# Weight splits of the experts without GpSimd, another order of the slots, and slots of 160 tokens, in a kernel of attention, a dense layer pair and a mixture of experts

## The chip, the cores and the metric

The kernel runs on one core of a Trainium2 chip, as one program. The metric is the time of one execution on the device in microseconds (us). The kernel before takes 613.17 us, the median of three runs (613.17, 613.51 and 611.21).

## The reference

Three layers run one after another, all in float32 with the dense layer's weights given in float64:

```python
scores = q @ k^T / 8, causal; attn = softmax(scores); x = attn @ v      # 2 x 12 heads, 448 tokens, 64 wide
x = x.reshape(896, 768)
y = (relu(x @ w_in) ** 2) @ w_out                                       # 768 -> 2048 -> 768
expert = argmax(normalized(y) @ normalized(expert_emb)^T / tau)         # one of 8 per token
gate   = softmax of the same logits, at the chosen expert
for e in range(8):
    out[expert == e] = gate * (relu(y[expert == e] @ w1[e]) @ w2[e])    # 768 -> 1024 -> 768
```

Which expert gets how many tokens is known only on the device.

## The kernel before

Products need more digits than one pass of TensorE gives, so every operand is kept as a high part (a rounded copy) and a low part (what the rounding left), and a product is made of three: high by high, high by low and low by high. The helper `copy_on` (L57 to L63) makes high parts, `lo_of` (L65, L66) low parts by a subtraction. Which engine does a class of them is a letter in the table `CFG`: A is ScalarE, V is VectorE, G is GpSimd; several letters go in turn by the piece's number.

Attention and the first dense layer take about the first half of the time. Then come seven tiles of 128 tokens of the second dense layer with their routing (`route_tile`), and as the last one goes on, the experts.

An expert's weights are 16 pieces of 128 x 768: pieces 0 to 7 for the first layer, 8 to 15 for the second. `pieces` loads two pieces at a time (768 KB, on SyncE's queue, into one of six buffers named `xraw` and `mraw`) and splits each into `mh` (high) and `ml` (low). All experts share one set of 16 slots for split pieces, so a piece of the next expert can be split only when TensorE has done with the same piece of the expert before, and its buffer is loaded again only when both parts are made. `CFG["mhi"]` names the engines of the high parts, `CFG["mlo"]` those of the low parts.

The tokens of an expert go into a slot of fixed size. The early slot (form D, 256 tokens) takes tokens of the expert that has most in the first five tiles; a slot of form M takes more of them with the same weights. After it come five static slots, `FORMS = "LMTTT"`, that hold 384 (L), 192 (M) and 64 (T) tokens, each with an expert's weights of its own, the larger ones for the experts with more tokens; `CFG["order"]` says in which order they are run. `tables` computes on the device which expert gets which slot and which token which lane. What does not fit goes to further slots of form L, which `rest` runs only if a flag says that there are tokens left.

`mm1_w` computes the first layer of forms D and M with the weights as the stationary operand, eight steps of 128 hidden units; in form M the moving operand is [high | low] of the tokens, so a step is six pairs of products (L703, L704), and VectorE then adds the two halves (`hsum`, L707) and makes the low part of the hidden layer (L712). `mm1_x` does form T (and the last third of L) with the tokens stationary: four steps of 256 hidden units; each result is added up by VectorE (`hr`, L774), transposed by TensorE (`ht`, L747), and becomes high and low part of the hidden layer (`act`, L749 on ScalarE, L750 on VectorE). `mm2` is the second layer, eight steps with two halves of 384 columns; a part with fewer than 128 tokens goes through `two_pass`, where high and low of the tokens lie side by side as one stationary operand. `mm2_out` weights the result by the gate (`osb`, L809 to L812), and GpSimd scatters it to the output with an indirect DMA (L814). `slot_x` gathers a slot's tokens (L826, GpSimd), transposes them (`xt`, L836) and splits them (`act`, L840 and L66).

The order of TensorE's work is written out by hand: `run_slot` calls hooks between the steps. On the other engines a scheduler orders the instructions when the program is built, and each engine works in that order.

Of the kernel before, what the change touches and what calls it, by code (L numbers as in the profile page):

```python
# [20 lines left out]
P = 128  # L21
# [11 lines left out]
def f32(ap):  # L33
# [5 lines left out]
    joint=1, mhi="AAAV", rt6=[1, 4, 7, 9, 15], woh="A", h2h="A", h2l="V", rt=[1, 3, 5, 7, 10], et=[9, 10, 14],  # L39
    turn2=[1, 3], ft0=[0, 1, 2, 3, 4], ft1=[3, 7], ft2=[2, 4, 5, 6], stop=0, mlo="VVGG", xh="A", h2="A",  # L40
# [4 lines left out]
    vh="AG", kl="G", vl="G", pth="AAAA", nrm="GGGGGGG", u0=1, order=[1, 2, 0, 3, 4])  # L45


def build(tc, qkd, vd, w_in, w_out, emb, tau, wm, cst, out, dbg_y=None):
# [24 lines left out]
    # causal, the same for rows 0 to 63 and 64 to 127  # L73
# [19 lines left out]
    # the activation tables come in while the first loads are under way  # L93
# [4 lines left out]
    # left: staging, slots of one f tile of weights, x (later phase B's tiles); right: attention (later h2)  # L98
# [8 lines left out]
    def w_load(src, f, slot, name, wh="wh", wl="wl", parts=1):  # L107
        """f tile of a float64 weight (as int64 words): float32 with 24 bits, then hi and lo"""
# [29 lines left out]
    # zeros that stay: beside the queries' blocks, beside v's second head, and after the even chunks  # L138
    # of the probabilities
# [29 lines left out]
    def s_prep(u):  # L169
        # rows 0 to 63: the first head of the pair; rows 64 to 127: the second  # L170
# [31 lines left out]
    # the chunks' order in each half unit  # L202
    COL = {c: i for i, c in enumerate(sum(sum(CFG["ch"], ()), ()))}

    def s_scores(u, c):
        """chunk c of the queries of both heads of a pair: the array's two diagonal blocks"""
# [27 lines left out]
    # the probabilities' transposes: blocks of 128 keys j, chunks of queries c >= 2 * j; a bank takes four  # L234
    BANKS = [[(0, c) for c in range(4)], [(0, c) for c in range(4, 7)] + [(3, 6)],
             [(1, c) for c in range(2, 6)], [(1, 6)] + [(2, c) for c in range(4, 7)]]
    # block j lies in half of them, from this chunk on
# [15 lines left out]
    def s_pv(u, j):  # L253
        """block j of the keys for both heads of a pair: the first gives rows 0 to 63, the second the others"""
# [55 lines left out]
    def scores_at(k):  # L310
        """the chunks of scores of half unit k, in three parts"""
        u = (k + 3) // 2
        return [[(units[u], c) for c in x] for x in CFG["ch"][(k + 1) % 2]] if 0 <= u < NU else [(), (), ()]
# [11 lines left out]
    # the array's clock rises with its work: products that nobody reads, while the pipeline fills  # L325
# [62 lines left out]
    def h2_split(t, q):  # L388
        """hi and lo of four f tiles of a token tile's h2, as [P, f, 128]"""
# [13 lines left out]
    # the next pieces of h2 go before the matrix products that they follow on DVE and ACT  # L403
# [27 lines left out]
    # phase B: y = h2 @ w_out for a tile of 128 tokens at a time, and its routing  # L431
# [8 lines left out]
    # unit-length expert embeddings, transposed, hi | lo  # L440
# [7 lines left out]
    def norm_of(pool, ss, n, name):  # L448
        """sqrt(ss) for [n, 1]: Newton's iteration for 1/sqrt on DVE"""
# [58 lines left out]
    def route_tile(t, y):  # L508
# [40 lines left out]
        # first of the maxima: least of (index - 8)  # L549
# [9 lines left out]
        # gate = 1 / (sum + 1e-9), in two parts  # L559
# [7 lines left out]
        # place among the tokens of its expert  # L567
# [8 lines left out]
    def lanes(rk, nt, name):  # L576
        """half and lane in a slot of 256, of ranks [P, nt]"""
# [6 lines left out]
    def table(oc, nt, nv, ncol, lane, name):  # L584
        """sum over tokens of (one-hot of the lane) x (one-hot of the column) * value"""
# [27 lines left out]
    def early():  # L613
        """the first 256 tokens of the expert with most tokens in the first NE tiles"""
# [30 lines left out]
    # the experts: pieces of [P, 768] of an expert's weights go round the 16 slots  # L645
# [9 lines left out]
    def h_at(fs, part, n, m=1):  # L655
        """hi and lo of the hidden layer of a part's n tokens (of m parts)"""
# [6 lines left out]
    def pieces(s, res):  # L663
        """the weights of an expert: 16 pieces, (hi, lo) each"""
# [21 lines left out]
    # forms of a slot: tokens of its parts. 64 tokens of one part lie with hi and lo side by side  # L686
# [39 lines left out]
    def two_pass(os, x, whs, wls, k, n):  # L726
        """x = [hi | lo] of 64 tokens: rows 0 to 63 of o get hi * (wh + wl), the others lo * wh"""
        def high():
            for o, w in zip(os, whs):
                T.matmul(o, x, w, start=(k == 0), stop=(k == n - 1))  # L730
# [368 lines left out]
NE = 5  # L1099
# [73 lines left out]
```

## Time and profile before

| | |
|---|---|
| Median of the runs | 613.17 us |
| Lowest and highest run | 611.21 and 613.51 us |
| Profiled execution: first to last instruction (span) | 610.8 us |
| Mean granted clock of TensorE | 0.968 of full |
| TensorE matmul busy | 568.2 us (93%) |
| TensorE weight loads busy (beside the matmuls) | 522.3 us (86%) |
| VectorE busy | 433.8 us (71%) |
| ScalarE busy | 274.0 us (45%) |
| GpSimd busy | 274.7 us (45%) |
| Bytes moved by DMA | 86.71 MB, 142 GB/s on average |

The profile gives the profiled execution as its span; what an execution has beyond that is not shown apart, and the lowest of the three runs lies 0.4 us above the span. Busy times are sums over the whole span, so they say nothing on which engine another waits for in a given stretch; for that one reads the windows, the timelines and the waits. In the rows PE is TensorE, PEld its weight loads, DVE VectorE, ACT ScalarE, POOL GpSimd and SP SyncE. L66 is line 66 of the kernel.

### The profile page before, as it was taken

To read this page: it belongs to the slowest core of one execution; us is meant where nothing else is said; L and a number is where in the kernel's file an instruction comes from. 1 tells how busy PE (TensorE), PEld (TensorE's weight loads), DVE (VectorE), ACT (ScalarE), POOL (GpSimd) and SP (SyncE) were. 2 spreads that over 40 slices of the span, in tenths; PEclk is the share of its full clock that TensorE was granted. 3 is DMA by queue.
4 is the path that set the end of the run, shared out by engine and by line. 5 is a ranking of instruction groups with operands and counts; after the bars stand their busy time and mean duration, and the time that the engine had idled before them with its cause. 6 is when DMAs were issued, how large, how long until landed. Compare 5 with 4: busy or idle time off the path is not lost. (4 is left out here: it accounts for less than half of the span.)

```text
span 610.8 us, 9820 instructions
## 1 busy us (share of the span) xinstructions
PE 568.2 (93%) x3501; PEld 522.3 (86%) x3501; DVE 433.8 (71%) x876; ACT 274.0 (45%) x630; POOL 274.7 (45%) x252
## 2 busy tenths in 40 slices
PE   6999999999999999999999988899898978999783
PEld 3788788899999989999999987899898957999663
DVE  6877778856779885976543779752988897265981
ACT  4776777424343425333332155103564654164541
POOL 7667577915554362210000055112574687054860
PEclk7999999999999999999999999899998969999788
DMA  7659433333364455411000192038486679047600
GB/s 223 161 134 256 112 66 93 126 105 104 103 207 156 155 166 198 156 53 52 27 27 10 34 407 94 2 133 308 155 268 212 228 240 296 3 141 257 206 1 6
DMA packets 28298, 86.71 MB, mean 142 GB/s; under 512 B 2854, under 2 KB 13094, under 8 KB 28240
## 3 DMA queue, kind: packets, MB, share of 16 engines
q1 hardware_dynamic: 26640, 79.51, 40.6%
q0 software_dynamic: 1600, 6.49, 2.9%
q8 instruction: 29, 0.48, 0.3%
q14 instruction: 29, 0.24, 0.1%
HBM read 75.44 MB, written 6.49 MB: 134 GB/s over the span
## 5 line engine op out<-in xcount | busy, mean ns | idle before, releaser
L66 POOL TENSOR_TENSOR ml<-xraw,mh 128x768 fp32r<-128x768 f32 x32 | 64.1, 2009 | 39.4 <-ACT mh L59 27.8
L215 PE MATMUL s<-kh,q 128*128 128x128 f32 (+6 forms) x168 | 51.5, 340 | 6.0 <-ACT p L219 4.5
L66 DVE TENSOR_TENSOR ml<-xraw,mh 128x768 fp32r<-128x768 f32 x32 | 48.7, 1522 | 11.7 <-ACT mh L59 11.6
L793 PE MATMUL ops<-mh,act 128*128 128x384 f32 x224 | 53.7, 342 | 0.0
L230 POOL TENSOR_SCALAR p<-p,rs 128x192 f32<-128x192 f32 (+6 forms) x84 | 43.4, 535 | 18.6 <-ACT p L219 12.7
L59 ACT ACTIVATE mh<-xraw 128x768 fp32r<-128x768 f32 x48 | 40.1, 844 | 21.9 <-PE ops L793 10.3
L264 PE MATMUL pv<-pt,v 128*128 128x448 f32 (+7 forms) x288 | 48.6, 304 | 0.0
L219 ACT ACTIVATE p<-s,mn 128x192 f32<-128x192 f32 (+6 forms) x84 | 39.6, 476 | 10.1 <-DVE mn L218 6.1
L123 DVE SCALAR_TENSOR_TENSOR w<-raw,w 128x768 int32<-128x768 int32 x32 | 43.1, 1350 | 0.7
L264 PEld LDWEIGHTS pv<-pt,v 128*128 128x128 f32 (+3 forms) x288 | 37.0, 163 | 5.2 <-issue 0.3
L215 PEld LDWEIGHTS s<-kh,q 128*128 128x128 f32 x168 | 33.8, 204 | 8.2 <-ACT p L219 5.4
L66 POOL TENSOR_TENSOR ml<-mraw,mh 128x768 fp32r<-128x768 f32 x16 | 33.2, 2082 | 15.3 <-ACT mh L59 10.6
L826 POOL DMA_INDIRECT xr<-ydram,egi x2 | 2.3, 1128 | 83.8 <-DVE esi L605 83.5
L793 PEld LDWEIGHTS ops<-mh,act 128*128 128x128 f32 x224 | 39.1, 188 | 0.3
L66 DVE TENSOR_TENSOR hs<-h,hs 128x512 fp32r<-128x512 f32 (+1 forms) x32 | 21.9, 691 | 24.7 <-ACT hs L59 24.5
L218 DVE TENSOR_REDUCE mn<-s 128x1 f32<-128x192 f32 (+6 forms) x84 | 34.1, 415 | 5.1 <-PE s L216 4.8
L121 DVE SCALAR_TENSOR_TENSOR w<-raw,w 128x768 int32<-128x768 int32 x32 | 36.0, 1128 | 0.7
L119 DVE TENSOR_SCALAR w<-raw 128x768 int32<-128x768 int32 x32 | 22.3, 698 | 18.8 <-POOL wi3l L66 6.7
L66 DVE TENSOR_TENSOR pt<-pt 128x512 fp32r<-128x512 f32 x48 | 32.4, 680 | 2.8 <-ACT pt L59 2.7
L294 ACT ACTIVATE relu<-pa 128x448 f32<-128x448 f32 x32 | 17.1, 538 | 36.6 <-PE pa L290 36.6
L703 PE MATMUL hps<-act,mh 128*128 128x384 f32 x96 | 29.5, 377 | 3.6 <-DVE hsum L707 3.6
L826 POOL DMA_INDIRECT xr<-ydram,fgi x10 | 12.0, 1197 | 44.9 <-DVE ei L999 23.5
(461 smaller groups left out, 1790.1 us busy)
## 6 DMA issues: line engine op xcount, KB each, us to landing
xraw<-in_wm SPq DMA_DIRECT2D x32, 768.0 KB, 4.5
raw<-in_w_in SPq DMA_DIRECT2D x16, 768.0 KB, 4.2
raw<-in_w_out SPq DMA_DIRECT2D x16, 768.0 KB, 4.2
mraw<-in_wm SPq DMA_DIRECT2D x16, 768.0 KB, 5.1
qk<-in_qkd SPq DMA_DIRECT2D x11, 448.0 KB, 5.2
q<-qs SPq DMA_DIRECT2D x22, 224.0 KB, 3.9
v<-in_vd SPq DMA_DIRECT2D x12, 256.0 KB, 4.1
ydram<-ysb SPq DMA_DIRECT2D x7, 384.0 KB, 2.3
```

The lines of the kernel that those rows point to most:

```text
L59: A.activation(out, in_, AF.Copy, scale=scale)
L66: eng.tensor_tensor(out=lo, in0=x, in1=hi, op=ALU.subtract)
L119: V.tensor_scalar(out=w[:, x], in0=raw[:, x, 1], scalar1=3, scalar2=0x3FFFFFFF, op0=ALU.logical_shift_left, op1=ALU.bitwise_and)
L121: V.scalar_tensor_tensor(out=w[:, x], in0=raw[:, x, 1], scalar=-0x40000000, in1=w[:, x], op0=ALU.bitwise_and, op1=ALU.bitwise_or)
L123: V.scalar_tensor_tensor(out=w[:, x], in0=raw[:, x, 0], scalar=29, in1=w[:, x], op0=ALU.logical_shift_right, op1=ALU.bitwise_or)
L215: T.matmul(ss, d["q2"][:, c, :, :, x].rearrange("p a b -> p (a b)"), d[y][:, :n], start=i == 0, stop=False)
L218: last["max"] = V.reduce_max(out=d["mn"][:, i:i + 1], in_=ss, axis=AX.X, negate=True)
L219: A.activation(d["p"][c][:, :n], ss, AF.Exp, bias=d["mn"][:, i:i + 1], accum_out=d["sm"][:, i:i + 1])
L230: G.tensor_scalar(out=p, in0=p, scalar1=rs[:, COL[c]:COL[c] + 1], scalar2=1.0, op0=ALU.mult, op1=ALU.mult)
L264: T.matmul(d["pv"][:, j * P:S] if h else d["pv"][0:D, j * P:S], d[x][0:k, j, 1:3].rearrange("p a b -> p (a b)") if h else d[x][0:k, j, 0], ...
L703: T.matmul(both, wh[:, c], mo["x"][:, kc, :, 0:n], start=(kc == 0), stop=False)
L793: T.matmul(ps[c], x, ww[:, c * 384:(c + 1) * 384], start=(fc == 0 and x is hh and ww is wh), stop=(fc == 7 and x is hl))
```

## The change

There are three edits, and nothing else that computes.

- Splits of the experts' weights: high parts (`mhi`) by ScalarE alone, where every fourth was VectorE's; low parts (`mlo`) by VectorE alone, where half were GpSimd's. GpSimd keeps the gathers and scatters of the experts.
- The static slots come in the order T, M, T, L, T, where it was M, T, L, T, T.
- Form M holds 160 tokens, where it held 192: its second part has 32 tokens instead of 64. `two_pass` and `mm2_out` take the number of tokens, the table of gates for the low rows is made for 32 as well as 64, and slot sizes are counted in units of 32.

```diff
-    joint=1, mhi="AAAV", ...
+    joint=1, mhi="A", ...
-    turn2=[1, 3], ..., stop=0, mlo="VVGG", xh="A", h2="A",
+    turn2=[1, 3], ..., stop=0, mlo="V", xh="A", h2="A",
-    vh="AG", kl="G", vl="G", pth="AAAA", nrm="GGGGGGG", u0=1, order=[1, 2, 0, 3, 4])
+    vh="AG", kl="G", vl="G", pth="AAAA", nrm="GGGGGGG", u0=1, order=[2, 1, 3, 0, 4])
...
-    FORM = dict(D=(P, P), M=(P, 64), S=(P,), T=(64,))
+    FORM = dict(D=(P, P), M=(P, 32), S=(P,), T=(64,))
...
-    def two_pass(os, x, whs, wls, k, n):
+    def two_pass(os, x, whs, wls, k, n, m):
         def high():
             for o, w in zip(os, whs):
-                T.matmul(o, x, w, start=(k == 0), stop=(k == n - 1))
+                T.matmul(o[0:2 * m], x, w, start=(k == 0), stop=(k == n - 1))
...
-            T.matmul(o[0:64], x[:, 0:64], w, start=False, stop=False)
+            T.matmul(o[0:m], x[:, 0:m], w, start=False, stop=False)
...
-                A.activation(oc, ps[c][64:P], AF.Copy, scale=s[1][3][64:P, col:col + 1])
-                V.scalar_tensor_tensor(out=oc, in0=ps[c][0:64], scalar=gate[0:64, col:col + 1], in1=oc,
+                A.activation(oc, ps[c][n:2 * n], AF.Copy, scale=s[1][3][n:2 * n, col:col + 1])
+                V.scalar_tensor_tensor(out=oc, in0=ps[c][0:n], scalar=gate[0:n, col:col + 1], in1=oc,
...
-        V.tensor_copy(gate2[64:P], gate[0:64])
+        for n in (64, 32):
+            V.tensor_copy(gate2[n:2 * n], gate[0:n])
...
-SIZE = dict(L=384, M=192, T=64)
+SIZE = dict(L=384, M=160, T=64)
+UNIT = 32
```

How the order moves shows on VectorE in a first small slot. Here is the order before, from the slot's first `hr` on (`ml<-xraw` is a low part of the next expert's weights, `CAST mh` a high part; a trailing x2 means two such rows):

```order
L66 TENSOR_TENSOR ml<-xraw,mh 128x768
L774 TENSOR_TENSOR hr<-hps,hr 64x256
L61 CAST mh<-xraw 128x768
L66 TENSOR_TENSOR ml<-xraw,mh 128x768
L774 TENSOR_TENSOR hr<-hps,hr 64x256
L66 TENSOR_TENSOR ml<-xraw,mh 128x768
L750 SCALAR_TENSOR_TENSOR act<-ht,act 128x2x64
L774 TENSOR_TENSOR hr<-hps,hr 64x256
L66 TENSOR_TENSOR ml<-xraw,mh 128x768
L61 CAST mh<-xraw 128x768
L750 SCALAR_TENSOR_TENSOR act<-ht,act 128x2x64
```

And now, in the first small slot, which follows the first slot of form M:

```order
L66 TENSOR_TENSOR ml<-mraw,mh 128x768
L774 TENSOR_TENSOR hr<-hps,hr 64x256
L66 TENSOR_TENSOR ml<-mraw,mh 128x768 x2
L774 TENSOR_TENSOR hr<-hps,hr 64x256
L66 TENSOR_TENSOR ml<-mraw,mh 128x768
L66 TENSOR_TENSOR ml<-xraw,mh 128x768
L750 SCALAR_TENSOR_TENSOR act<-ht,act 128x2x64
L774 TENSOR_TENSOR hr<-hps,hr 64x256
L66 TENSOR_TENSOR ml<-xraw,mh 128x768 x2
L750 SCALAR_TENSOR_TENSOR act<-ht,act 128x2x64
```

Between two of the instructions that TensorE's transposes and products need (`hr`, `act<-ht`) there are now two low parts, where there were one low part and now and then a cast.

The second place is VectorE in the first layer of the slot of form M that has weights of its own. Before:

```order
L707 TENSOR_TENSOR hsum<-hps,hsum 128x192
L66 TENSOR_TENSOR ml<-mraw,mh 128x768
L712 SCALAR_TENSOR_TENSOR act<-hsum,act 128x128
L712 SCALAR_TENSOR_TENSOR act<-hsum,act 128x64
L66 TENSOR_TENSOR ml<-mraw,mh 128x768
L707 TENSOR_TENSOR hsum<-hps,hsum 128x192 x2
L61 CAST mh<-mraw 128x768
L712 SCALAR_TENSOR_TENSOR act<-hsum,act 128x128
L712 SCALAR_TENSOR_TENSOR act<-hsum,act 128x64
L712 SCALAR_TENSOR_TENSOR act<-hsum,act 128x128
```

And now, where that slot follows a small one, from the last piece of its own weights on:

```order
L66 TENSOR_TENSOR ml<-mraw,mh 128x768
L707 TENSOR_TENSOR hsum<-hps,hsum 128x160
L66 TENSOR_TENSOR ml<-xraw,mh 128x768 x2
L707 TENSOR_TENSOR hsum<-hps,hsum 128x160
L712 SCALAR_TENSOR_TENSOR act<-hsum,act 128x128
L712 SCALAR_TENSOR_TENSOR act<-hsum,act 128x32
L66 TENSOR_TENSOR ml<-xraw,mh 128x768
L712 SCALAR_TENSOR_TENSOR act<-hsum,act 128x128
L712 SCALAR_TENSOR_TENSOR act<-hsum,act 128x32
L66 TENSOR_TENSOR ml<-xraw,mh 128x768
```

The first `hsum` now comes behind the last low part of the slot's own weights, and low parts of the slot after it stand between the others.

The third place is GpSimd over the same slots. Before:

```order
L826 DMA xr<-ydram,fgi 64x768
L66 TENSOR_TENSOR ml<-xraw,mh 128x768
L826 DMA xr<-ydram,fgi 128x768
L66 TENSOR_TENSOR ml<-xraw,mh 128x768
L814 DMA out<-osb,fsi 896x768
L66 TENSOR_TENSOR ml<-xraw,mh 128x768
L814 DMA out<-osb,fsi 896x768
L66 TENSOR_TENSOR ml<-mraw,mh 128x768 x2
L66 TENSOR_TENSOR ml<-xraw,mh 128x768 x2
L826 DMA xr<-ydram,fgi 128x768
```

And now:

```order
L827 DMA xr<-ydram,fgi 64x768
L827 DMA xr<-ydram,fgi 128x768
L815 DMA out<-osb,esi 896x768
L827 DMA xr<-ydram,fgi 32x768
L815 DMA out<-osb,fsi 896x768 x2
L827 DMA xr<-ydram,fgi 64x768
L827 DMA xr<-ydram,fgi 128x768
L815 DMA out<-osb,fsi 896x768
```

Only gathers (`xr<-ydram`) and scatters (`out<-osb`) are left.

## Rows read from the trace of the kernel before

**Rows 1.** Windows by slot: length; busy PE, PEld, DVE, ACT, POOL; clock; DMA; GB/s.

```profile
422.30:453.20 30.90, 29.28 (x189) 28.04 (x189) 24.53 (x38) 17.70 (x43) 15.79 (x10) 1.00 0.58 184
453.20:485.50 32.30, 30.35 (x185) 29.12 (x184) 27.36 (x39) 17.19 (x42) 18.74 (x12) 0.95 0.70 229
485.50:510.30 24.80, 18.98 (x102) 15.47 (x100) 24.38 (x24) 14.74 (x27) 22.24 (x12) 0.79 0.77 252
510.30:563.80 53.50, 53.18 (x382) 52.47 (x381) 25.94 (x32) 20.44 (x38) 21.22 (x13) 1.00 0.47 160
563.80:587.90 24.10, 17.51 (x96) 14.44 (x95) 22.68 (x20) 13.38 (x24) 19.29 (x11) 0.81 0.44 152
587.90:601.50 13.60, 13.41 (x89) 11.41 (x87) 7.54 (x14) 4.02 (x11) 4.68 (x3) 0.97 0.01 2
```

**Rows 2.** Timeline of TensorE: start, duration, instruction, count, idle before and its releaser.

```profile
434.33 0.44 PE L703 MATMUL hps<-act,mh 128*128 128x384 f32 x1 [1.62 <-DVE hsum L707]
...
437.83 0.54 PE L793 MATMUL ops<-mh,act 128*128 128x384 f32 x2
...
465.71 0.53 PE L703 MATMUL hps<-act,mh 128*128 128x384 f32 x1 [1.95 <-DVE hsum L707]
...
470.80 0.53 PE L793 MATMUL ops<-mh,act 128*128 128x384 f32 x2
...
570.84 0.33 PE L747 MATMUL ht<-ident,hr 64*128 64x64 f32 x2 [3.00 <-DVE hr L774]
```

**Rows 3.** Timeline of VectorE and GpSimd, 565 to 586 us.

```profile
565.64 4.82 DVE L66 TENSOR_TENSOR ml<-mraw,mh 128x768 fp32r<-128x768 f32 x1 [0.54 <-ACT mh L59]
...
565.99 1.89 POOL L66 TENSOR_TENSOR ml<-xraw,mh 128x768 fp32r<-128x768 f32 x1
...
570.38 0.41 DVE L774 TENSOR_TENSOR hr<-hps,hr 64x256 f32<-64x256 f32 x1
...
583.99 0.94 DVE L66 TENSOR_TENSOR ml<-xraw,mh 128x768 fp32r<-128x768 f32 x1
...
584.86 0.55 DVE L61 CAST mh<-xraw 128x768 fp32r<-128x768 f32 x1
...
585.48 1.85 POOL L66 TENSOR_TENSOR ml<-xraw,mh 128x768 fp32r<-128x768 f32 x1 [2.44 <-DVE mh L61]
```

**Rows 4.** Groups by form, 422.3 to 604 us: busy, mean ns; idle, releasers.

```profile
L66 DVE TENSOR_TENSOR ml<-xraw,mh 128x768 fp32r<-128x768 f32 x26 | 40.8, 1570 | 11.3 <-ACT mh L59 11.2
...
L59 ACT ACTIVATE mh<-xraw 128x768 fp32r<-128x768 f32 x39 | 32.4, 842 | 20.1 <-PE ops L793 10.3 <-PE ops L730 5.1 <-issue 2.8
...
L66 DVE TENSOR_TENSOR ml<-mraw,mh 128x768 fp32r<-128x768 f32 x14 | 28.0, 2010 | 2.5 <-ACT mh L59 2.3
...
L712 DVE SCALAR_TENSOR_TENSOR act<-hsum,act 128x128 fp32r<-128x128 f32 x16 | 13.3, 828 | 0.1
...
L826 POOL DMA_INDIRECT xr<-ydram,fgi x6 | 8.0, 1334 | 19.1 <-PE xt L836 18.5 <-issue 0.5
...
L812 DVE SCALAR_TENSOR_TENSOR osb<-ops,fgate,osb 64x384 f32<-64x384 f32 x10 | 5.7, 602 | 4.1 <-ACT osb L811 4.1
...
L707 DVE TENSOR_TENSOR hsum<-hps,hsum 128x192 f32<-128x192 f32 x16 | 5.3, 351 | 5.7 <-ACT hsum L706 5.3
...
L774 DVE TENSOR_TENSOR hr<-hps,hr 64x256 f32<-64x256 f32 x12 | 4.8, 406 | 0.3 <-ACT hr L773 0.2
...
L750 DVE SCALAR_TENSOR_TENSOR act<-ht,act 128x128 fp32r<-128x128 f32 x12 | 3.4, 281 | 2.3 <-ACT act L749 2.2
```

**Rows 5.** Timeline of TensorE, first layer of the first 192-token slot.

```profile
424.26 0.36 PE L703 MATMUL hps<-act,mh 128*128 128x384 f32 x1
424.46 0.25 PE L704 MATMUL hps<-act,ml 128*128 128x192 f32 x1
424.54 0.36 PE L703 MATMUL hps<-act,mh 128*128 128x384 f32 x1
```

**Rows 6.** Windows view, the 10 us with the fastest transfers.

```profile
410.00:420.00 10.00, 8.95 (x56) 8.30 (x55) 1.67 (x3) 2.49 (x5) 3.03 (x3) 1.00 0.99 364
```

More of the change, by code (lines that the diff above doesn't have):

```diff
@@ L38 @@
     first=1, rt5=[1, 3, 4, 5, 8], hp=3000, xe=[1, 10, 11, 12, 13], turn=5, xfd=[3, 4, 5, 6], xfj=[1, 2, 3, 4],
-    joint=1, mhi="AAAV", rt6=[1, 4, 7, 9, 15], woh="A", h2h="A", h2l="V", rt=[1, 3, 5, 7, 10], et=[9, 10, 14],
-    turn2=[1, 3], ft0=[0, 1, 2, 3, 4], ft1=[3, 7], ft2=[2, 4, 5, 6], stop=0, mlo="VVGG", xh="A", h2="A",
+    joint=1, mhi="A", rt6=[1, 4, 7, 9, 15], woh="A", h2h="A", h2l="V", rt=[1, 3, 5, 7, 10], et=[9, 10, 14],
+    turn2=[1, 3], ft0=[0, 1, 2, 3, 4], ft1=[3, 7], ft2=[2, 4, 5, 6], stop=0, mlo="V", xh="A", h2="A",
     wh="G", wil="G", wol="GV", warm=6, nsa=6, nwi=3, nwb=3, wo0=4, hs0=[4, 5, 8, 9], conv0=17, convs=2, pin=1,
@@ L765, in mm1_x @@
                 else:
-                    two_pass([ps], xh[:, kc, 0:P], [wh[:, c]], [wl[:, c]], kc, KC)
+                    two_pass([ps], xh[:, kc, 0:P], [wh[:, c]], [wl[:, c]], kc, KC, n)
             if q % 2 == 0:
@@ L795, in mm2 @@
                     else:
-                        two_pass([ps[c] for c in cs], mo["h"][:, fc, part, 0:P],
-                                 *([x[:, c * 384:(c + 1) * 384] for c in cs] for x in (wh, wl)), fc, 8)
+                        m = FORM[s[0]][part]
+                        two_pass([ps[c] for c in cs], mo["h"][:, fc, part, 0:2 * m],
+                                 *([x[:, c * 384:(c + 1) * 384] for c in cs] for x in (wh, wl)), fc, 8, m)
         for (s, part), ps in zip(parts, pss):
@@ L833, in slot_x @@
                 yield
-                xt = ps_h.tile([P, 512], F32, tag="h", name="xt")[:, :384].rearrange("p (a b) -> p a b", b=n)
+                xt = ps_h.tile([P, 512], F32, tag="h", name="xt")[:, :nk * n].rearrange("p (a b) -> p a b", b=n)
                 for j in range(nk):
@@ L937, in tables @@
         V.reduce_sum(out=cap, in_=zc, axis=AX.X)
-        V.tensor_scalar(out=cap, in0=cap, scalar1=-64.0, scalar2=float(CAP), op0=ALU.mult, op1=ALU.add)
+        V.tensor_scalar(out=cap, in0=cap, scalar1=-float(UNIT), scalar2=float(CAP), op0=ALU.mult, op1=ALU.add)
         over = small([NZ], "over")
@@ L1101 @@
 FORMS = "LMTTT"
-SIZE = dict(L=384, M=192, T=64)
+SIZE = dict(L=384, M=160, T=64)
+UNIT = 32
 CAP = SIZE["L"]
-STEPS = [i + 1 for i, f in enumerate(FORMS) for _ in range((SIZE[f] - SIZE.get(FORMS[i + 1:i + 2], 0)) // 64)]
+STEPS = [i + 1 for i, f in enumerate(FORMS) for _ in range((SIZE[f] - SIZE.get(FORMS[i + 1:i + 2], 0)) // UNIT)]
 NSS = len(FORMS)
```

## The prediction

> **What bounds the kernel now.** The page's busy shares say little, since the change touches only the stage after 350 us. So I cut the experts' stretch into its six slots, each from its first product on TensorE to the next slot's first [rows 1]. Call them C (the 192-token slot that goes on with the early slot's weights), M (the 192-token slot with weights of its own), T1, L, T2 and T3, in today's order. The reader is to see two kinds. In L and T3 TensorE is busy nearly throughout: they are at their floor. In T1 and T2 it works 18.98 of 24.8 us and 17.51 of 24.1 us, part of that at the lower clock (the clock column gives 0.79 and 0.81), while VectorE is busy nearly all the time. T3 does the same products in 13.6 us: no expert follows it, so nothing is split beside it. So a small slot costs some 10 us more when the next expert's weights are split during it. C and M each lose about 2 us in the same way, M some more by the clock.
>
> Next I asked what TensorE waits for. Every stall of over 1 us between 423 and 602 us, save one of 1.77 us, ends with a VectorE instruction; three are shown [rows 2]. Then, what VectorE did just before. The timeline ahead of the 3.00 us stall tells it [rows 3]: a low part (`ml`, the subtraction in `lo_of`, L66) that is put down at 4.82 us begins just before GpSimd starts low parts of its own, and ends long after; only then comes the `hr` that TensorE wants. At 584 us, with GpSimd between two low parts, the same subtraction is put down at 0.94 us, and the next VectorE instruction starts 0.87 us later. The table of groups says the same on average: 40 low parts on VectorE at 1570 and 2010 ns; 16 hidden-layer low parts (L712, a sixth of the size) at 828 ns [rows 4]. So VectorE is full of waiting for GpSimd rather than of work.
>
> **The change, part by part.** The sum is made on the profiled execution, whose span is 610.8 us; the runs' median of 613.17 us stands 2.4 us above it, and I carry differences over.
>
> *The splits.* Today an expert's 16 pieces cost GpSimd 8 low parts, VectorE 8 low parts and 4 high parts, ScalarE 12 high parts. Then: VectorE 16 low parts, ScalarE 16 high parts. At 0.87 us from start to start an expert takes VectorE 13.9 us; ScalarE, at 842 ns [rows 4], 13.5 us. These lie beside TensorE as long as what TensorE waits for is not behind them in VectorE's order, and the order shows that it is: in a small slot each `hr` and each `act<-ht` stands behind two or three low parts of the next expert. I followed that chain from TensorE's first product in T1. VectorE has a leftover of two gated outputs (602 ns each, which first need ScalarE) and one low part, the 16th of the slot's own; then comes the next expert's first low part, which ends at 4.7 us, and the first `hr` (406 ns [rows 4], some 0.34 us from start to start), at 5.05. TensorE has done its 34 products (0.12 us each) by 4.1, stands at the transpose and waits 1 us. The second `hr` is there at 7.15 (two low parts later), 0.35 us late. The first `act` comes after two more, at 9.1, and the second layer waits 1.45 us. From there each two of its eight steps (1.4 us of products) stand against two low parts, an `hr` and an `act<-ht` (281 ns), 2.3 us; it ends at 17.5 us. I take 18, for some loss of clock. Bounds: 13.6 us, T3's length, if the chain hides; 23.5 us if the clock stays down as now.
>
> *The order.* It is now C, T, M, T, L, T. Two of three small slots still have an expert after them, as before, so by itself this moves no wait; it lets the 192-token slot follow a small one. There VectorE starts with some 6 us of leftover (five low parts, three `act<-xt`, two outputs), and four of the first layer's steps wait 0.6 to 1.4 us for `hsum`, in all 2.9 us. Bounds 0 and 4.
>
> *160 instead of 192 tokens.* In the first layer a pair of products (384 and 192 columns) starts every 0.28 us [rows 5]; it becomes 320 and 160. By columns it would be 0.233; if only the larger product shrinks (0.20 x 5/6, and 0.08 as it is), 0.247. I take 0.24: 48 pairs save 1.9 us per slot, bounds 1.6 and 2.3. The second layer moves the same 384 columns of weights past fewer stationary ones and I leave it as it is. The tokens fit: counted from the reference's inputs, the experts have 143, 1, 0, 387, 360, 0, 3 and 2 tokens; of 387 the early slot takes 256, and 131 and 143 are under 160, 360 is under 384. No slot of the part behind a flag is run.
>
> *The early slot.* Its 16 pieces are split from 354 to 383 us, beside the last tiles' routing. VectorE gets 8 low parts more and loses 4 casts and the waits for GpSimd; I take 0, bounds -2 and +3 us.
>
> *GpSimd.* It keeps the gathers and scatters, which no longer queue behind low parts; nothing waits longer for them, so 0. A gather takes 1334 ns to issue [rows 4]; were that doubled, six in this stretch would come 8 us later in all, but the order issues each a slot ahead of its transposes. The Trainium skill (SBUF — State Buffer, section SBUF: two separate sides) warns that VectorE can keep GpSimd from writing a DMA's descriptors while it runs a copy that uses both ports. By that rule the busier VectorE would delay them and the sum would take up to those 8 us more; of such copies the trace shows the casts of the high parts, and the change takes these from VectorE.
>
> *Sum.* C: 30.9 less 1.9 (columns) less 1.6 (its stall) plus 0.7 (a new, shorter one) is 28. M: 32.3 less 1.9, less its 1.95 stall, less 1.6 (the 24 products after the stall took 5.09 us, in C 3.50 us [rows 2]), plus 2.9, is 29.8; I write 29.5, since one piece of VectorE's leftover may come earlier. T1 and T2: 18 each. L 53.5, T3 13.5. Together 160.5 against 179.2 us: 18.7 us less. 613.17 - 18.7 is **594.5 us**. Set against occupancy: from C to the second T VectorE would have 64 x 0.87 us of low parts and some 27 us of other work (an estimate: 16 `hsum`, 32 L712, 8 `hr`, 8 `act<-ht`, 8 `osb` and 9 `act<-xt` at their rows' times without GpSimd), 83 us, in 93.5 us, and TensorE 82 us of products; two engines as full as that don't hide each other wholly, which is why I don't take less.
>
> **Rivals.**
> *All hidden.* If the new stalls vanish (C and M at their 29.3 us of products less 1.9, T1 and T2 at 13.6, L 53.5, T3 13.5), the six take 149 us: 30.2 us less, 583 us. For it: 13.9 us of low parts fit into the 26 us of a larger slot. Against: VectorE's order.
>
> *The clock stays down.* The granted clock is 0.95 in M and 0.81 in T2, with stalls of 1.95 and 3.00 us, and 1.00 in C, with one of 1.62 us [rows 1, 2]. My stalls in T1 are 0.35 to 1.45 us, but there are six in 17 us. With T1 and T2 at 23.5 and M at 31, the six take 173 us: 607 us.
>
> *The low parts stay long, and VectorE becomes the bound: slower.* If what stretches them is not GpSimd but, say, the DMA that fills `xraw` beside them, 16 go on taking 1.72 us (the mean of the 40 [rows 4]), 27.5 us per expert. From C to the second T that is 110 + 27 = 137 us of VectorE where the three slots C, M and T1 take 88.0 now and the second T 24.1; with L and T3 the six take 204 us, 25 us more: 638 us. It decides from 64 x + 27 = 112, so x = 1.33 us: above it the change loses. Against it stands the 0.94 us with GpSimd between two low parts [rows 3], in a slot whose transfers run at 152 GB/s [rows 1]. The Trainium skill (Perfetto Trace Analysis, section Optimizing Scalar/DVE Operations) says that a saturated VectorE is a reason to move work to ScalarE or even to GpSimd, while adding that GpSimd shares a read port with it; the first half speaks against this change, and by it the time would lie on this side.
>
> *An extra slot.* If a count were over 160, a whole further slot with its weights not loaded ahead would be run at the end, some 60 us: 655 us. The counts above exclude it unless the kernel routes tokens in another way than the reference.
>
> *Weights as the bound.* A slot's 6.3 MB (8 loads of 768 KB) take 17.3 us at 364 GB/s, the most that a stretch of 10 us shows [rows 6]. A small and a 160-token slot together are 47 us for two experts, so transfers would have to run at 268 GB/s. I keep it as part of the upper half of the range, not as a case.
>
> **Chances.** Forecast (588 to 600 us) 0.55; all hidden 0.17; clock 0.13; no change to speak of, because new stalls eat the gain (610 to 616), 0.07; slower by VectorE or an extra slot 0.08. The range of 582 to 606 us takes in the first three but for their outer edges, some 0.8. A measurement can tell about 0.5% (3 us) from no change: faster 0.85, same 0.07, slower 0.08.
>
> **What would show it.** Right: low parts on VectorE at 0.95 us throughout, 96 of them; GpSimd with DMA issues only after 350 us; small slots of 17 to 19 us with stalls under 1.5 us that end with `hr` or `act` on VectorE; pairs of the 160-token slot 0.24 us apart. Wrong: low parts over 1.3 us; small slots of 14 us (all hidden) or over 22 us with the clock column near 0.8; stalls that end with a DMA; a branch taken into a further slot.

## The result, and the profile after

The changed kernel takes 590.75 us (median of four runs, 588.62 to 592.21), the kernel before in the same comparison 612.27 us (four runs, 611.21 to 613.51). The ratio is 0.9643 with a 95% interval of 0.9614 to 0.9672: 3.6% faster. A later comparison of the same two kernels gave 589.70 against 612.01 us, ratio 0.9641 (0.9614 to 0.9668). The profiled execution has a span of 590.5 us where the one before had 610.8.

The page's busy times of the changed kernel:

```profile
PE 562.6 (95%) x3501; PEld 516.5 (87%) x3501; DVE 399.0 (68%) x901; ACT 291.8 (49%) x654; POOL 192.3 (33%) x204
```

VectorE took over GpSimd's half of the low parts, and yet is busy for 399.0 us, 34.8 us less than before. What it gave away doesn't explain that: 24 casts at 0.55 us [rows 3] are 13 us, and the 48 low parts that it took on are 46 us at today's 951 ns. That is the first sign that its busy time before was to a good part waiting.

The windows by slot, cut as in [rows 1], in the new order C, T1, M, T2, L, T3 (columns as there):

```profile
423.40:450.55 27.15, 27.15 (x184) 25.11 (x182) 18.52 (x40) 18.90 (x44) 1.95 (x2) 1.00 0.62 196
450.55:468.50 17.95, 14.92 (x101) 12.17 (x100) 17.00 (x29) 16.79 (x30) 11.52 (x4) 1.00 0.87 310
468.50:497.00 28.50, 27.46 (x182) 25.26 (x183) 22.12 (x45) 19.97 (x46) 7.11 (x3) 1.00 0.86 296
497.00:516.30 19.30, 17.37 (x102) 14.52 (x101) 17.35 (x29) 16.93 (x31) 9.74 (x4) 0.82 0.88 314
516.30:569.40 53.10, 53.09 (x382) 52.44 (x381) 24.50 (x37) 23.84 (x42) 2.86 (x3) 1.00 0.28 91
569.40:582.50 13.10, 13.09 (x90) 11.14 (x88) 4.32 (x11) 5.04 (x13) 1.98 (x2) 1.00 0.14 56
```

The six slots take 159.1 us instead of 179.2, so 20.1 us of the span's 20.3 come from here. (C starts 1.1 us later, and what follows the last product is 1.3 us shorter.) The two small slots gave 6.85 and 4.8 us, C and M 3.75 and 3.8. L and T3, which were at their floor, moved little. In T2 TensorE has the lower clock in part (a granted clock of 0.82 on average), in T1 not.

Groups by form, 423.4 to 584 us (columns as in [rows 4]):

```profile
L66 DVE TENSOR_TENSOR ml<-xraw,mh 128x768 fp32r<-128x768 f32 x52 | 48.8, 951 | 15.5 <-ACT mh L59 15.5
L59 ACT ACTIVATE mh<-xraw 128x768 fp32r<-128x768 f32 x52 | 43.2, 844 | 17.0 <-PE ops L730 9.9 <-PE ops L793 4.9 <-PE hps L703 2.0
L66 DVE TENSOR_TENSOR ml<-mraw,mh 128x768 fp32r<-128x768 f32 x28 | 26.3, 950 | 14.4 <-ACT mh L59 14.4
...
L815 POOL DMA_INDIRECT out<-osb,fsi x9 | 23.4, 2602 | 76.1 <-ACT osb L810 63.9 <-DVE hr L774 5.8 <-DVE osb L813 3.5
...
L827 POOL DMA_INDIRECT xr<-ydram,fgi x6 | 10.7, 1787 | 38.6 <-PE xt L837 38.6
...
L712 DVE SCALAR_TENSOR_TENSOR act<-hsum,act 128x128 fp32r<-128x128 f32 x16 | 4.5, 283 | 0.1
```

A low part on VectorE now takes 951 and 950 ns in both buffers, where it took 1570 and 2010. L712, which no edit touches, fell from 828 to 283 ns. VectorE's idle time now ends with ScalarE's high part.

TensorE's waits (timeline; the bracket is the idle time before and what ended it):

```profile
375.15 0.17 PE L556 MATMUL rk<-OH,tri 128*128 128x8 bf16 x1 [2.80 <-DVE OH L553]
...
411.03 0.52 PE L837 MATMUL xt<-ident,xr 128*128 128x128 f32 x3 [3.30 <-DMA xr<-ydram,fgi]
455.11 0.34 PE L747 MATMUL ht<-ident,hr 64*128 64x64 f32 x2 [0.38 <-DVE hr L774]
457.18 0.39 PE L730 MATMUL hps<-mh,act 128*128 128x256 f32 x1 [1.35 <-DVE hr L774]
459.11 0.33 PE L747 MATMUL ht<-ident,hr 64*128 64x64 f32 x2 [0.50 <-DVE act L750]
...
465.58 0.55 PE L837 MATMUL xt<-ident,xr 32*128 32x32 f32 x6 [0.69 <-DVE act L750]
...
477.55 0.39 PE L703 MATMUL hps<-act,mh 128*128 128x320 f32 x1 [1.03 <-DVE hsum L707]
...
503.65 0.39 PE L730 MATMUL hps<-mh,act 128*128 128x256 f32 x1 [1.35 <-DVE hr L774]
```

From C on no wait is over 1.35 us; before, there were waits of 1.62, 1.95 and 3.00 us [rows 2] and more like them. The first three in T1 are those that the prediction read off VectorE's order; the fourth, of 0.69 us, it did not have. The two largest now stand ahead of C: 2.80 us for the routing of the sixth of the seven tiles, whose small operations stand between the early slot's low parts in VectorE's order, and 3.30 us for the gather of C's tokens. The kernel before waited there too, three times for the routing and once for the gather:

```profile
363.27 0.53 PE L529 MATMUL lgt<-yhl,ent 128*16 128x256 f32 x3 [1.13 <-DVE ynt L458]
367.74 0.29 PE L535 MATMUL lg<-ident,lgs 16*128 16x16 f32 x2 [1.82 <-DVE sc L538]
...
384.05 0.82 PE L529 MATMUL lgt<-yhl,ent 128*16 128x256 f32 x3 [2.79 <-DVE ynt L458]
...
411.46 0.52 PE L836 MATMUL xt<-ident,xr 128*128 128x128 f32 x3 [1.05 <-DMA xr<-ydram,fgi]
```

### The profile page after: what moved, and what is told of

It is laid out like the page before. It is cut to its first block, busy times and chain, and to the rows that moved or that the text cites. A ratio compares the mean times of both kernels' runs of the same rounds, so it can differ in the third digit from the quotient of the medians.

```text
span 590.5 us, 9782 instructions
## 1 busy us (share of the span) xinstructions
PE 562.6 (95%) x3501; PEld 516.5 (87%) x3501; DVE 399.0 (68%) x901; ACT 291.8 (49%) x654; POOL 192.3 (33%) x204
## 4 chain that ended last, share of the span: by engine, by line
PE 85%; DVE 6%; DMA 3%; ACT 3%; issue 2%; SPq 0%; POOL 0%; POOLq 0%; DVEq 0%; ACTq 0%
PE yps L496 19%; PE ops L793 9%; PE pa L289 7%; PE pa L290 7%; PE pa L288 7%; PE pv L264 6%; PE s L215 6%; PE pt L247 4%; PE hps L703 3%; DVE ml L66 3%; PE hps L719 2%; PE hps L718 2%; PE ops L735 2%; PE hps L720 2%; PE ops L730 2%
## 5 line engine op out<-in xcount | busy, mean ns | idle before, releaser
L66 DVE TENSOR_TENSOR ml<-xraw,mh 128x768 fp32r<-128x768 f32 x64 | 60.2, 951 | 19.2 <-ACT mh L59 19.0
L59 ACT ACTIVATE mh<-xraw 128x768 fp32r<-128x768 f32 x64 | 53.4, 845 | 19.0 <-PE ops L730 9.9
L215 PE MATMUL s<-kh,q 128*128 128x128 f32 (+6 forms) x168 | 53.4, 352 | 4.4 <-ACT p L219 4.3
L815 POOL DMA_INDIRECT out<-osb,fsi x10 | 24.3, 2433 | 85.5 <-ACT osb L810 63.9
L827 POOL DMA_INDIRECT xr<-ydram,fgi x10 | 14.7, 1467 | 92.3 <-DVE fsi L605 49.8
L215 PEld LDWEIGHTS s<-kh,q 128*128 128x128 f32 x168 | 35.4, 215 | 6.5 <-ACT p L219 4.9
L66 DVE TENSOR_TENSOR ml<-mraw,mh 128x768 fp32r<-128x768 f32 x32 | 30.1, 950 | 14.8 <-ACT mh L59 14.8
L247 PE MATMUL pt<-ident,p 128*128 128x128 f32 x192 | 32.1, 284 | 0.0
L59 ACT ACTIVATE mh<-mraw 128x768 fp32r<-128x768 f32 x32 | 26.7, 844 | 9.5 <-PE ops L793 3.7
```

Source lines behind the costliest of these rows:

```text
L59: A.activation(out, in_, AF.Copy, scale=scale)
L66: eng.tensor_tensor(out=lo, in0=x, in1=hi, op=ALU.subtract)
L215: T.matmul(ss, d["q2"][:, c, :, :, x].rearrange("p a b -> p (a b)"), d[y][:, :n], start=i == 0, stop=False)
L247: T.transpose(pt[:, o * P:(o + 1) * P], d["p"][c][:, j * P:(j + 1) * P], ident)
```

## The experiments

### Which edit did it

**The splits alone**, on the kernel before:

```diff
-    mhi="AAAV", ... mlo="VVGG",
+    mhi="A", ... mlo="V",
```

> The kernel before with the splits alone changed (high parts by ScalarE, low parts by VectorE); order M, T, L, T, T and 192 tokens as before. Theory (GpSimd's low parts stretched VectorE's, and that was the loss): low parts on VectorE at 0.95 us on average, both inner small slots 18 to 19 us instead of 24, the 192-token slots free of stalls over 1.2 us; the 160-token form is worth some 1.2 us per slot by the trace after (a pair of products every 0.26 us against 0.28), so the time is 612.3 - 21.5 + 2.5, about 593 us, 590 to 597. Rival (the new order of the slots gives most of the gain): 603 us or more.

Measured: 590.09 us (588.57 to 590.69), ratio 0.9635 (0.9597 to 0.9673): as much as the whole change. Groups by form of this kernel:

```profile
L66 DVE TENSOR_TENSOR ml<-xraw,mh 128x768 fp32r<-128x768 f32 x52 | 48.9, 951 | 24.9 <-ACT mh L59 24.9
...
L66 DVE TENSOR_TENSOR ml<-mraw,mh 128x768 fp32r<-128x768 f32 x28 | 26.2, 951 | 5.7 <-ACT mh L59 5.6
```

The split of the time over the small slots is not the one expected: the first took 19.76 and the second 15.73 us, where 18 to 19 was expected of both.

**The order alone**, on the kernel before (`order=[2, 1, 3, 0, 4]`):

> The kernel before with the order of the static slots alone changed, to T, M, T, L, T. Theory: two of three small slots are still followed by an expert whose weights are split beside them, so each of these two keeps its 24 us and the time stays within 3 us of the kernel before, 609 to 615 us. Rival (order gives most): 600 us or less.

Measured: 613.03 us (609.86 to 616.95), ratio 1.0003 (0.9976 to 1.003). No difference in the total. Low parts still took 1705 and 1254 ns on VectorE, and the stalls of 3.3 us stood in the small slots as before. Within the total the order does move time: the two small slots took 27.5 and 26.2 us, where 24 was expected, with new waits of 3.58 and 3.50 us ahead of the transposes of the next slot's tokens, and C and M came out 0.6 and 2.0 us shorter than before.

**160 tokens alone** (old splits, old order):

> The kernel before with slots of 160 tokens alone: GpSimd keeps half of the low parts, the order is M, T, L, T, T. Theory: 96 pairs of products start 0.02 us sooner each, about 2 us, and the stalls of the two larger slots stay because VectorE is still held by GpSimd: 608 to 612 us. Rival (TensorE's columns were the larger part of the gain): below 605 us.

Measured: 609.96 us (605.42 to 613.37), ratio 0.9963 (0.9934 to 0.9991), some 2 us. VectorE's low parts took 1569 and 1987 ns, the stalls were 1.84, 2.26, 3.23 and 2.94 us: the waits are not touched.

**The change with the old order**:

```diff
-    order=[2, 1, 3, 0, 4])
+    order=[1, 2, 0, 3, 4])
```

> The changed kernel with the order of the slots as before (M, T, L, T, T). Theory: the order is worth nothing by itself, so the same as the changed kernel within 3 us, 588 to 594 us; the two small slots that have an expert after them take 18 to 19.5 us, the last 13. Rival (small slots between larger ones let the transfers or VectorE catch up): 596 us or more, with two small slots side by side taking over 34 us, or stalls that end with a DMA.

Measured: 590.39 us (586.45 to 591.89), ratio 0.9624 (0.9573 to 0.9675). The order is worth nothing with the new splits either. As in the kernel with the splits alone, the small slots are not as expected one by one: 19.70, 15.72 and 14.01 us, in the changed kernel 17.95, 19.30 and 13.10.

This kernel differs from that of the splits alone only in the 160 tokens, and the medians don't show these. The slots do: C's first layer (96 products) takes 12.56 us here and 13.86 there, so a pair starts every 0.26 instead of 0.29 us; C is 1.28 us shorter, M 0.74. Ahead of C it is the other way round. C starts at 423.61 us here and at 419.79 there, at a clock of 0.89 against 1.00 between 375 and 390 us and of 0.87 against 1.00 between 412 and 425 us (the kernel with the splits alone has its lower level between 400 and 412 us, 0.86, where TensorE waits anyway), though the gather is waited for about as long (3.39 and 3.28 us). Why the lower clock falls otherwise in the two was not settled.

### Whether it is GpSimd that stretches VectorE

**GpSimd reads beside VectorE again.** In the changed kernel GpSimd makes half of the low parts a second time, in strips of 256 columns, into a tile that nobody reads:

```diff
+                if k % 4 >= 2:
+                    junk = spool.tile([P, 256], BF16, tag="junk", bufs=1, name="junk")
+                    for c in range(0, DM, 256):
+                        lo_of(G, junk, x[:, c:c + 256], f32(hi)[:, c:c + 256])
```

> The changed kernel, in which GpSimd makes the low part of every third and fourth piece a second time, in three strips, into a small tile that nobody reads; VectorE and ScalarE do all that they do in the changed kernel, and no engine waits for the copy except where a weight slot or a buffer comes free. Theory (it is GpSimd's reading beside it that stretches VectorE's subtractions): low parts on VectorE go from 0.95 us to 1.4 us or more on average, the small slots before another expert to over 23 us, and the time to 610 us or more, above the kernel before, since VectorE now has twice as many. Rival (the gain came from low parts being made sooner, or from where they are made, not from a quiet GpSimd): low parts stay under 1.1 us and the time within 5 us of 590.75.

Measured: 622.16 us (619.72 to 623.33), ratio 1.0167 (1.0126 to 1.0207), 31 us above the changed kernel though VectorE's instructions are the same. Groups by form of this kernel from 423 to 584 us, GpSimd's strips and VectorE's low parts:

```profile
L66 POOL TENSOR_TENSOR junk<-xraw,mh 128x256 bf16<-128x256 f32 x66 | 72.3, 1095 | 8.8 <-issue 4.2
L66 DVE TENSOR_TENSOR ml<-xraw,mh 128x768 fp32r<-128x768 f32 x49 | 58.7, 1213 | 16.8 <-ACT mh L59 16.8
```

The mean of 1213 ns (1138 in the other buffer) stayed under the 1.4 us that the theory asked for, but it stands against 951 in the changed kernel, and the page gives VectorE 430.1 us of busy time instead of 399.0 for the same 901 instructions. So GpSimd's strips do stretch VectorE's instructions. The small slots took 25.7 and 24.5 us, as the theory had it.

The time is less clear. TensorE's two longest waits, the first of a small slot and the second of M:

```profile
478.70 0.84 PE L841 MATMUL xt<-ident,xr 32*128 32x32 f32 x6 [4.44 <-DVE act L754]
498.15 0.60 PE L707 MATMUL hps<-act,mh 128*128 128x320 f32 x1 [6.67 <-DVE hsum L711]
```

Ahead of both, VectorE stood idle for over 3 us until ScalarE had made a high part, and ScalarE had waited for the weights themselves:

```profile
476.22 0.84 ACT L59 ACTIVATE mh<-xraw 128x768 fp32r<-128x768 f32 x1 [5.21 <-DMA xraw<-in_wm]
...
493.43 0.84 ACT L59 ACTIVATE mh<-xraw 128x768 fp32r<-128x768 f32 x1 [5.00 <-DMA xraw<-in_wm]
```

A load is issued when its buffer is free, and here the strips hold the buffers: between 425 and 600 us loads waited 17 times for a strip, 105 us in all. ScalarE's high parts waited 20.4 us for loads in this kernel, and not once for a load in the experts' slots of the changed kernel or of the kernel before (there they waited for TensorE's products [rows 4], though loads waited for GpSimd's low parts, 66.8 us). So a part of the 31 us is late weights, which this experiment adds and which the kernel before did not have; how large a part was not separated. The strips also both read and write, and which of the two stretches VectorE is not told apart.

**A quarter of the low parts on GpSimd** (`mlo="VVVG"` in the changed kernel):

> The changed kernel with every fourth low part given back to GpSimd (VVVG): per expert 12 on VectorE and 4 on GpSimd. Theory (GpSimd's reading stretches VectorE's instructions by about its own length): VectorE saves 4 x 0.87 = 3.5 us per expert and loses about 4 x 1.4 us to waiting, so the small slots before another expert get 1 to 3 us longer and stalls of over 1.9 us come back: 594 to 604 us, with low parts on VectorE at 1.2 to 1.4 us on average. Rival (VectorE is full in these slots, and work taken from it pays more than the contention costs): 589 us or less.

Measured: 589.57 us (588.04 to 590.04), ratio 0.9621 (0.9581 to 0.9661). Neither the theory's range nor the rival's holds this. The theory had the direction of the slots right: the small ones took 20.75 and 20.0 us instead of 17.95 and 19.30, and C's start to T2's end 95.2 us against 92.9 in the changed kernel. It had the sizes too large: low parts on VectorE took 1121 and 1172 ns, and the longest stall was 1.36 us, so none of over 1.9 us came back. What it had left out is the early slot. TensorE's waits there:

```profile
373.53 0.17 PE L556 MATMUL rk<-OH,tri 128*128 128x8 bf16 x1 [0.52 <-DVE OH L553]
...
405.69 0.52 PE L837 MATMUL xt<-ident,xr 128*128 128x128 f32 x3 [0.74 <-DMA xr<-ydram,fgi]
```

With four low parts of the early slot on GpSimd TensorE waits 0.52 instead of 2.80 us for that routing (and 1.32 us for the next tile's) and 0.74 instead of 3.30 for the gather; C starts at 416.47 instead of 423.38, 6.9 us earlier. Most of this is lost again: 2.3 us up to T2's end, 1.1 in L and 1.4 behind the last product; the spans are 588.3 and 590.5 us.

**Every fourth high part on VectorE** (`mhi="AAAV"` in the changed kernel):

> The changed kernel with every fourth high part on VectorE again (AAAV), GpSimd still without splits. VectorE gets 4 casts of 0.55 us per expert more, ScalarE 4 of 0.84 us less. Theory (with GpSimd quiet, VectorE's amount of work sets the small slots and the slot after them): 1 to 2 us more in each of four slots, 592 to 598 us. Rival (ScalarE, busy for 16.8 of 18 us in a small slot, is the one that sets it): 587 us or less.

Measured: 597.17 us (595.49 to 599.43), ratio 0.9754 (0.9709 to 0.9799). The casts take their proper time; VectorE simply has more to do, and the wait for the second `hr` grows from 1.35 to 1.82 us. The theory has the total right, but not where it lies: T1 is 2.4 us longer, C 0.9 and L 0.7, M and T2 are not, and C starts 1.85 us later. TensorE's row in the first small slot:

```profile
460.11 0.38 PE L730 MATMUL hps<-mh,act 128*128 128x256 f32 x1 [1.82 <-DVE hr L774]
```

The group of the casts:

```profile
L61 DVE CAST mh<-xraw 128x768 fp32r<-128x768 f32 x13 | 7.2, 552 | 1.3 <-PE hps L703 0.9 <-PE ops L730 0.2
```

So of the two letters the low parts' is the larger one: with the old letter for the high parts the kernel is still 15 us faster than the kernel before, and the letter of the high parts is worth another 6.4 us (597.17 less 590.75).

### What bounds it now

**Second-layer pieces later.** The second half of M's and L's pieces is issued behind the first sums of their own slot, so that fewer low parts stand ahead of `hr` and `act` in the small slots:

```diff
+                    for ins in behind:
+                        es.enter_context(tc.issue_after(ins.ins))
...
+            if ps[0][0] in "DM":
+                for _ in range(4):
+                    next(it)
+                late = second(it)
```

> The changed kernel, in which the second layer's eight pieces of the 160-token slot with own weights and of the 384-token slot are split behind the first sums of that slot's first layer instead of at the end of the small slot ahead of it and before the first sum. VectorE's work is the same. Theory (what is left of the loss is VectorE's order: low parts of the next expert ahead of what TensorE waits for): each of the two small slots loses two to three low parts from its chain and the 160-token slot its stall of 1 us on hsum, 1.5 to 2.5 us each, so 584 to 588 us. Rival (VectorE is full over these slots, and what is moved comes back as a wait later): 589 to 593 us.

Measured: 593.45 us (592.49 to 596.05), ratio 0.9706 (0.9673 to 0.9739): the rival's time, a little over its range. T1 became 1.1 us shorter (16.81), T2 not (19.33), and M 6.1 longer (34.62). M's waits for `hsum` went from 1.03 to 5.3 us in all, these two among them:

```profile
476.07 0.39 PE L717 MATMUL hps<-act,mh 128*128 128x320 f32 x1 [1.15 <-DVE hsum L721]
481.26 0.61 PE L717 MATMUL hps<-act,mh 128*128 128x320 f32 x1 [3.43 <-DVE hsum L721]
```

Moved away from one wait, the work makes a longer one. The rival's reason, that VectorE is full there, holds for T1 of the changed kernel (17.00 of 17.95 us busy) but not for M (22.12 of 28.50), so why M pays that much was not settled.

**The early slot's side work one step later.** In the changed kernel the last routing, the tables and C's transposes are called between the steps of the early slot's products; one call is dropped, so that all after it comes later and TensorE has products left while the gather is under way:

```diff
-    ft1=[3, 7],
+    ft1=[3],
```

> The changed kernel with the hook for the continued slot's first transposes moved from the last step of the early slot's first part to the third step of its second part, so that the gathered tokens have three more steps (3 x 1.06 us) to arrive. In the changed kernel TensorE waits there 3.3 us for the gather and then runs 19 products in 4.9 us, which the kernel before did in 3.4 us. Theory: the wait and the lower clock behind it go, 3 to 5 us, so 586 to 588 us. Rival (the time comes back, since VectorE's tables or the split of the next weights start from the same place): 589 to 592 us.

Measured: 584.07 us (582.94 to 590.41), ratio 0.9554 (0.9509 to 0.9600). The wait for the gather:

```profile
410.17 0.52 PE L837 MATMUL xt<-ident,xr 128*128 128x128 f32 x3 [0.26 <-DMA xr<-ydram,fgi]
```

That is more than the theory had. C starts at 417.83 us instead of 423.38, 5.5 us earlier, for 3.0 us of wait: the clock is 1.00 between 412 and 425 us, where the changed kernel has 0.87 after its long wait, and 0.9 us were there already when the gather was issued (403.83 against 404.77), at a clock of 0.89 against 0.78 between 375 and 390 us.

**The same with a quarter of the early slot's low parts on GpSimd**, and the changed kernel beside it:

```diff
-                lo_of(ENG[CFG["mlo"][k % len(CFG["mlo"])]], lo, x, f32(hi))
+                mlo = "VVVG" if s[0] == "D" else CFG["mlo"]
+                lo_of(ENG[mlo[k % len(mlo)]], lo, x, f32(hi))
```

> The kernel with one step of transposes after seven tiles moved (the run before this in the text), and GpSimd making every fourth low part of the early slot alone; all other slots as in the changed kernel. If what the quarter on GpSimd gave was the early stage alone (the wait for rk 0.5 us instead of 2.8) and the small slots keep VectorE to themselves: C starts near 415.5 us, small slots 18 to 19.5 us, 580 to 583 us. If the early stage's gain was the transposes' wait for the gather, which is already gone here, nothing is left: 583 to 586 us.

> The changed kernel itself, for a comparison with the kernels above on the same chip: 589 to 592 us, a ratio of 0.962 to 0.967 to the kernel before.

Measured: 586.78 us (585.71 to 587.53), ratio 0.9595 (0.9568 to 0.9622); the changed kernel 589.70 us (588.81 to 590.44). The first is outside both ranges. C started at 415.36 us as forecast, but T2 took 20.5 and L 54.2 us. The edit reached further than its text: the first two parts of L have form D as well, so GpSimd got four low parts of L's expert, which are made in T2 and L. VectorE's timeline in T2 of this kernel:

```profile
495.69 3.00 DVE L66 TENSOR_TENSOR ml<-mraw,mh 128x768 fp32r<-128x768 f32 x1
```

And GpSimd's at the same time:

```profile
493.63 2.37 POOL L816 DMA_INDIRECT out<-osb,fsi  x1 [2.95 <-DVE hr L775]
496.03 1.84 POOL L66 TENSOR_TENSOR ml<-xraw,mh 128x768 fp32r<-128x768 f32 x1
```

One low part on GpSimd, and VectorE's low part beside it takes 3.00 us; the transpose behind it then waits 1.89 us instead of 0.20 in the changed kernel. This is [rows 3] over again in a kernel where nearly all else is clean, and the most direct sight of the mechanism.

**In the early slot alone** (`if s[1] is etabs`):

> As the kernel before it in the text, but with GpSimd's quarter in the early slot alone (there the edit also reached the slot for 384 tokens, whose first two parts have the same form: four of its low parts went to GpSimd, one beside a low part of VectorE's that took 3.00 us). If those four gave the early gain back, the early slot's gain stays: C starts near 415.4 us as there, T2 takes 18 to 19.5 us instead of 20.5, the 384-token slot 53.1 instead of 54.2, in all 580.5 to 583.5 us. If the gain is given back whoever makes them (the weights' transfers are the bound), 584 to 586 us.

Measured: 584.62 us (581.25 to 587.00), ratio 0.9530 (0.9492 to 0.9568). The median lies in the rival's range, the single runs on both sides of it. C starts at 415.17 us and L takes 53.1 us again, as the theory has it. Windows of T1 and T2 in this kernel:

```profile
442.34:461.71 19.37, 17.24 (x102) 14.04 (x101) 17.37 (x29) 16.78 (x30) 9.78 (x4) 0.82 0.90 309
...
490.14:509.51 19.37, 17.24 (x101) 14.38 (x101) 17.39 (x29) 16.98 (x31) 9.70 (x4) 0.82 0.89 310
```

The first stalls in T1 are those of the changed kernel (0.38, 1.35 and 0.41 us), yet the clock is 0.82 instead of 1.00, and the slot takes 1.4 us more. So half of the 2.7 us gained ahead of C is gone by the start of M, while the transfers in T1 run as fast as in the changed kernel (309 and 310 GB/s): it is the clock that gave it back there, not the transfers that the rival names. The medians of this kernel and of the one with the transposes later alone can't be told apart. Both beat the changed kernel by 5 to 7 us and the kernel before by 4.5 and 4.7%.

## Why the prediction was right

Forecast 594.5 us (582 to 606), measured 590.75, 3.75 us less. The six slots give 1.4 us of that; 1.5 us more is that the profiled execution, to which they belong, took 592.21 us and was the slowest of the four. Point by point:

| Term | Forecast | Measured, profiled execution |
|---|---|---|
| C | 28.0 | 27.15 |
| M | 29.5 | 28.50 |
| T1 | 18.0 | 17.95 |
| T2 | 18.0 | 19.30 |
| L | 53.5 | 53.10 |
| T3 | 13.5 | 13.10 |
| Sum of the six | 160.5 | 159.10 |
| Start of C against before | 0 (-2 to +3) | +1.1 |
| After the last product against before | none | -1.3 |

- **VectorE waits for GpSimd rather than works.** Right. 951 ns in every buffer after, and the rival by which transfers keep the low parts long, up to 638 us, is out: they run at 310 GB/s in T1, twice the 152 GB/s of the row that the rival was weighed by, with the low parts still at 951 ns. That it is GpSimd is shown from the other side by the repeated low parts (951 ns became 1213) and by the 3.00 us low part beside a single one of GpSimd's. What it cost the kernel shows in the runs that change the letters, 22 us with both (590.09) and 15 where only the low parts moved (597.17, with the new order and 160 tokens); the 31 us of the repeated low parts hold late weights as well. The Trainium skill (Perfetto Trace Analysis, section Optimizing Scalar/DVE Operations) gives a saturated VectorE as a reason to move work to GpSimd; here the move the other way gave 2.5% (ratio 0.9754), and 3.6% together with that of the casts to ScalarE, so for this pair of engines the measurement decides against that half of the sentence and for its caution that such a move might not help. The runs show the stretching; they don't show that a port is its reason.
- **The chain in a small slot.** T1 fits to 0.05 us, which is in part luck. The forecast was 17.5 us and 0.5 for the clock, and the clock stayed at 1.00; and the single stalls don't fit: forecast 1.0, 0.35 and 1.45 us, measured 0.38, 1.35 and 0.50, and one of 0.69 for a transpose that the forecast didn't have. The forecast had the right low parts in between and put their wait at the wrong one of the instructions.
- **T2** was taken as equal to T1. Its stalls are no longer, but its granted clock is 0.82 where T1's is 1.00. That is the clock rival at a small fraction of its 607 us.
- **160 tokens.** Mis-sized: a pair every 0.26 us, where 0.24 was taken, and in C 1.3 us and in M 0.7 where 1.9 was taken for each. By columns the larger product should shrink by a sixth; its mean fell from 360 ns in the kernel with the splits alone to 348.
- **M's stall** of 2.9 us for `hsum` was 1.03, and C's new one of 0.7 did not come. That outweighs what the columns failed to give: M came out 1.0 us below its term and C 0.85. The estimate of VectorE's work from C to the second T, 83 us, was too high as well: the four windows add up to 75.0 us. It was a reason for not forecasting less and no term of the sum.
- **The early slot** was costed at nothing. In the sum nearly so (+1.1 us), but not in its parts. The routing's waits fell from 1.13, 1.82 and 2.79 us to the one of 2.80, and the last routing was done 3.2 us sooner; the gather's wait grew from 1.05 to 3.30 us, since it took 6.3 us from its issue to the first transpose where it took 4.5, for a reason that was not settled; and the clock was 0.78 instead of 0.89 between 375 and 390 us and 0.87 instead of 1.00 between 412 and 425. The gather's wait is also a stall that ends with a DMA, one of the signs that the prediction named for being wrong; it lies ahead of the six slots. The later kernels show that some 5 us could be had there.
- **The order** was said to move no wait by itself. The total bears that out (1.0003), the slots don't: alone it lengthened the small ones by some 2 to 3 us and shortened C and M. With the new splits C is 0.6 us shorter than in the old order (27.15 against 27.80, with 184 products in it against 189), and the sum took nothing for that.
- **GpSimd** was costed at nothing, and from C on nothing waits for its gathers or scatters. Its issues did become longer, which the next section but one tells.

## What to carry to other kernels

Before a busy engine is taken for a full one, compare the same instruction's duration where the neighbour engine works and where it doesn't; the one row of 0.94 us among means of 1.57 and 2.01 carried this whole forecast. Work taken away from a neighbour can make the engine that receives it faster, so the sum needs the duration without the neighbour. And when a wait is removed, look ahead of the stage as well: here the next 5 us lay in the early slot, in one line of a hand-written order.

## What was not expected

Some of GpSimd's indirect DMAs became slow to issue where VectorE runs low parts one behind the other. GpSimd's timeline in T2 of the changed kernel:

```profile
497.68 1.02 POOL L815 DMA_INDIRECT out<-osb,fsi  x1 [8.16 <-ACT osb L810]
501.63 6.73 POOL L815 DMA_INDIRECT out<-osb,fsi  x1 [2.94 <-DVE hr L774]
513.29 1.04 POOL L827 DMA_INDIRECT xr<-ydram,fgi  x1 [4.93 <-PE xt L837]
515.35 1.39 POOL L827 DMA_INDIRECT xr<-ydram,fgi  x1 [1.02 <-PE xt L837]
```

And VectorE's as the second of them begins (three more pairs of low parts follow in the same way):

```profile
501.45 1.81 DVE L66 TENSOR_TENSOR ml<-xraw,mh 128x768 fp32r<-128x768 f32 x2
503.18 0.41 DVE L774 TENSOR_TENSOR hr<-hps,hr 64x256 f32<-64x256 f32 x1
```

A scatter that takes 1.02 us to issue four microseconds earlier takes 6.73 while VectorE runs low parts back to back; in T1 it was 6.76, and a gather took 4.62. It is not so wherever VectorE has no gap: the two gathers at 513 and 515 us took 1.04 and 1.39 us while it went on with low parts and splits of tokens (`act<-xt`) in turn. The Trainium skill (SBUF — State Buffer, section SBUF: two separate sides) warns of this for VectorE's copies that use both ports. What runs here are subtractions of two tiles, so the trace shows long issues beside more than the copies of that warning. From C on no product waits for a gather or a scatter, so no wait shows a cost; in a kernel whose gathers are needed sooner there could be one. Which of VectorE's operations do it was not tried alone.

The second thing is the clock. The changed kernel was profiled twice. Its T2 had the same two first stalls in both executions (0.38 and 0.37 us, 1.35 and 1.35), and took 19.30 us at a granted clock of 0.82 in the first and 17.85 us at 0.90 in the second:

```profile
496.34:514.19 17.85, 16.12 (x102) 13.82 (x101) 16.91 (x28) 16.93 (x31) 9.05 (x4) 0.90 0.87 310
```

T1 took 17.95 us at 1.00 in the changed kernel and 19.37 us at 0.82 in the last one. A small slot's time can therefore not be forecast to better than 1.4 us from its stalls, and the runs of one kernel spread over 2 to 8 us.
